# W1 by four casting transfers of the GpSimd queue, w sent to all partitions, one PSUM pool, free order of the second product, stores on two queues, and a new written order

## The chip, the cores and the metric

The kernel runs on one core of one Trainium2 chip. A core has five engines with an instruction stream each: TensorE (PE, matmuls and transposes into PSUM), VectorE (DVE), ScalarE (ACT), GpSimd (POOL) and SyncE (SP, which here only issues DMA transfers). Sixteen DMA engines move data between HBM and SBUF; transfers are issued by SP, ACT and POOL, each on a queue of its own. The metric is device time in microseconds for one execution, as the median of several runs; smaller is better.

## The reference

Two layers run one after the other. The first is a linear attention with a decaying state, for 4 batches, 8 heads, 768 steps and 48 channels per head:

```
state = 0                                       # (B, H, D, D)
for t in range(768):
    cur   = (u * k_t) outer v_t
    y_t   = r_t @ (state + cur)
    state = w * state + k_t outer v_t           # w: one factor per head and channel
```

The second takes the 3072 rows of 384 numbers that result, and computes

```
h   = max(x @ w_in, 0)                          # w_in: 384 x 2048, called W1 here
out = (h * h) @ w_out                           # w_out: 2048 x 384, called W2 here
```

All inputs and the output are float32 in HBM.

## The kernel before, in words

**Blocks.** The time axis is cut into chunks of 128 steps. A block i is one chunk of one batch (batch i % 4, chunk i // 4), 24 in all. In a block the decay is put into scaled copies of r and k, so that the loop becomes matrix products. These are the steps of block i, by the names that the code and the written order use:

- `ld.r.i`, `ld.k.i`, `ld.v.i`: loads, 192 KB each, in rows of 48 floats (192 bytes).
- `rh`, `kh`: r and k times powers of w, to bfloat16 (`Wt`, `Wk` are these powers, from `logw`). `P0`, `P1`, `du`, `dv`: the term with u (r times k, times u, summed per head, times v). `vb`: v in bfloat16.
- The transposed r and k come in one of two ways: `T` (eight transposes on PE into a PSUM bank) and `Tc` (a copy to SBUF), or `XB`, one transposing DMA issued by SP.
- `A`: scores, eight matmuls into two banks; `Bm.i.0`, `Bm.i.1`: masked copies; `Y`: scores times v plus (from chunk 1 on) r times the state; `xs`: Y plus the u term, to bfloat16.
- `U`: the update of the state; `S0`, `ts`, `S`: the state itself.
- x is transposed for the second layer either by `X` (PE) and `xTc` (a copy), or by `xX`, a transposing DMA on SP.

**Groups.** The second layer works on groups of blocks: group 0 is block 0, group 1 is block 1, group 2 is blocks 2 and 3, group 3 is 4 and 5, and so on to group 12. `F1.g.s` is one bank of the first product for group g (for two blocks: 6 matmuls of 256 columns, s from 0 to 7; for one block 12 matmuls of 128 columns, s from 0 to 3). `re` (relu) empties the bank, `sq` squares. `F2.i.q` is a quarter q of the second product for block i: 4 matmuls of 384 columns into the block's bank. `os` copies the finished bank to SBUF, `out` stores it.

**Weights.** W1 lies in SBUF as eight pieces of 256 columns, W2 as four pieces (q). `lW.0.s` loads a float32 piece of W1 on SP into one of four staging buffers, `cW.0.s` casts it (on ACT, one on POOL). `W.0.2` and all of W2 (`W.1.q`) come by a DMA that casts on its way, which POOL issues. In most pieces two neighbouring rows of W2 lie together, with the columns of W1 permuted to match. `w` sends the decay to four partitions, and `shw` on DVE spreads it to all 128.

**What sets the order.** Nothing is scheduled by a tool. `ORDER` is a list written out by hand: a step such as `F1.1.0:P/0` names what, the engine (P, D, A, G for POOL, S) and the buffer numbers. Each engine runs its own steps strictly in the order of the list, and waits where an input is missing or a buffer is still in use. `Z.n.b` are n filler matmuls on PE. The transfers issued by SP and ACT share eight semaphores in turn, so that each waits until the transfer eight places before it in the list has landed. The eight PSUM banks are fixed in three pools: 4 for the attention, 2 for F1, 2 for F2's results.

The lines touched are in `POOLS`, `ORDER`, `HELD`, `bank`, `weights`/`rows2`, `w`/`shw`, `lW`/`cW`/`W`, `F1`, `re`, `sq`, `F2` and `os`.

Of the kernel before, what the change touches and what calls it, by code (L numbers as in the profile page):

```python
# [18 lines left out]
POOLS = dict(ldr=7, ldk=7, ldv=7, ws=0, wsa=4, rk=7, P0=5, dv=5, vb=8, rkT=7, bank=4, bankH=2, bankO=2, Bm=6, xs=5, xT1=2, xT2=3, xT4=1, hr=6, hq=30, os=4, ts=2)  # L19
ORDER = """  # L20
ld.r.1:S/0 w:A ld.k.1:S/0 u:S Z.48.5:P tab:A ld.k.0:S/1 ld.k.2:S/2 shw:D ld.r.0:S/1 logw:A ld.r.2:S/2 Wt:A/0 P0.1:D/0
Wk:A/1 lW.0.6:S/0 kh.1:D/0 ld.v.1:S/0 rh.1:D shu:D ld.k.3:S/3 T.1:P/0 kh.0:D/1 Z.16.5:P P1.1:G Tc.1:A/0 kh.2:D/2
rh.0:D ld.v.3:S/1 WtS:A rh.2:D P0.2:G/1 A.1:P/1/2 WkS:A T.0:P/3 lW.0.1:S/1 Z.16.5:P P1.2:D ld.r.3:S/3 Tc.0:A/1
du.1:D/0 P0.0:D/2 cW.0.6:A ld.v.0:S/2 A.0:P/0/3 dv.1:G Bm.1.1:D/0 Z.6.5:P du.2:D/1 T.2:P/2 P1.0:G Bm.1.0:D/1
ld.v.2:S/3 Z.22.5:P Tc.2:A/2 Bm.0.0:D/2 Bm.0.1:D/3 lW.0.0:S/2 vb.1:A/0 lW.0.5:S/3 kh.3:D/3 Y.1:P/1 cW.0.1:A lW.0.7:S/0
A.2:P/0/2 xs.1:D/0 Z.4.5:P P0.3:G/3 vb.3:A/1 du.0:D/2 lW.0.4:S/1 X.1:P/3 Z.8.5:P rh.3:D wc:S xTc.1:A/0 Bm.2.0:D/4
vb.0:A/2 T.3:P/1 ld.k.4:S/4 dv.0:D Y.0:P/3 Z.13.5:P Tc.3:A/3 vb.2:G/3 Bm.2.1:D/5 P1.3:G xs.0:D/1 A.3:P/0/2 X.0:P/1
cW.0.0:A U.0:P/3 dv.2:G Bm.3.0:D/1 Z.6.7:P xTc.0:A/1 du.3:D/3 lW.0.3:S/2 F1.1.0:P/0 Bm.3.1:D/0 ld.r.4:S/4 F1.0.0:P/1
re.1.0:D/0 cW.0.7:G Y.2:P/0 Y.3:P/1 re.0.0:A/1 ld.k.5:S/5 xs.2:D/2 cW.0.5:A W.1.0:G dv.3:D F1.1.3:P/0 cW.0.4:A W.0.2:G
X.2:P/2 F1.0.3:P/1 re.1.3:D/2 ld.r.5:S/5 xTc.2:A/0 W.1.1:G U.2:P/0 xs.3:D/3 F1.0.2:P/0 re.0.3:A/3 sq.1.3:D2/0 WLcol:A  # L30
X.3:P/2 F1.1.2:P/1 re.0.2:D/4 xTc.3:A WLm:G U.3:P/1 F1.2.1:P/0 re.1.2:A/5 W.1.2:G sq.0.3:A0/1 F1.2.5:P/1 re.2.1:D/2
W.1.3:G sq.0.0:A0/2 U.1:P/2 S0.2:D re.2.5:A/3 F1.2.4:P/0 sq.0.2:D2/3 cW.0.3:A S0.0:D F1.2.7:P/1 re.2.4:D/1 sq.1.0:A0/4
F2.0.0:P/1 sq.2.5:D2/5 re.2.7:A/4 S0.3:D F1.0.1:P/0 F1.2.3:P/1 re.0.1:D/0 F2.1.0:P/0 S0.1:D re.2.3:A/3 F1.1.1:P/0
sq.1.2:D2/6 sq.0.1:D2/7 ld.k.7:S/6 F1.2.0:P/1 re.1.1:A/5 F2.0.1:P re.2.0:A/0 sq.1.1:D2/8 F1.2.2:P/0 sq.2.4:A0/9
sq.2.0:D1/10 F2.1.1:P kh.4:D/4 F1.2.6:P/1 ld.v.5:S/4 rh.4:D P0.4:D/4 F2.1.2:P ld.r.7:S/6 re.2.2:D/5 P1.4:G F2.0.2:P
re.2.6:D/1 sq.2.2:A0/11 F2.1.3:P ld.v.4:S/5 kh.5:G/5 sq.2.1:A0/12 sq.2.6:D1/13 F2.0.3:P os.1:A/0 du.4:D/4 ld.k.6:S/0
T.4:P/0 sq.2.3:A0/14 rh.5:D F2.2.0:P/0 os.0:A/1 P0.5:D/0 Tc.4:A/4 ld.r.6:S/0 T.5:P/3 P1.5:D F2.2.1:P kh.7:D/6 Tc.5:A/5
ld.v.7:S/6 A.4:P/1/2 du.5:D/0 F2.3.0:P/1 Bm.4.0:D/3 ld.k.9:S/2 A.5:P/0/3 vb.4:A/4 dv.4:G Bm.4.1:D/2 F2.3.1:P vb.5:A/5
ld.r.9:S/2 Bm.5.1:D/4 dv.5:G sq.2.7:A0/15 Y.4:P/1 Bm.5.0:D/5 F2.3.2:P rh.7:G ld.k.8:S/1 xs.4:D/4 U.4:P/2 Y.5:P/3
F2.2.2:P P0.6:G/1 ld.v.6:S/0 xs.5:D/0 X.4:P/0 ts.4:D/0 X.5:P/1 T.7:P/3 xTc.4:A/1 kh.6:D/1 ld.k.15:S/3 F2.2.3:P xTc.5:A  # L40
rh.6:D vb.7:A/6 U.5:P/2 P1.6:D F1.3.0:P/0 Tc.7:A/6 ld.k.10:S/4 ts.5:D/1 F1.3.1:P/1 kh.9:D/2 re.3.0:A/0 ld.v.9:S/2
T.6:P/0 P0.7:D/2 os.2:A/2 A.7:P/1/2 S.5:D re.3.1:A/5 ld.r.8:S/1 F2.3.3:P du.6:D/2 P1.7:G Tc.6:A/0 Bm.7.1:D/0
F1.3.3:P/0 sq.3.0:A0/16 rh.9:G ld.r.10:S/3 os.3:D/3 F1.3.4:P/1 re.3.3:A/2 Bm.7.0:D/1 A.6:P/3/0 P0.9:G/3 du.7:D/1
re.3.4:A/1 XB.9:S/1 F1.3.5:P/0 Bm.6.1:D/3 sq.3.1:A0/17 dv.7:G F1.3.6:P/1 Bm.6.0:D/2 re.3.5:A/3 F2.5.0:P/0 dv.6:G
vb.6:A/7 ld.k.12:S/5 sq.3.3:A0/18 Y.7:P/2 out.3:S kh.10:D/3 re.3.6:A/4 Y.6:P/1 ld.v.8:S/3 S.4:G xs.7:D/1 F1.3.2:P/0
sq.3.5:A0/19 xs.6:D/2 F1.3.7:P/1 ld.v.11:S/1 kh.8:D/0 re.3.2:A/0 kh.15:D/4 U.6:P/0 X.6:P/3 sq.3.2:A0/20 X.7:P/2 rh.8:D
F2.4.0:P/1 ld.r.12:S/4 re.3.7:A/5 rh.10:D F2.5.1:P xTc.6:A/2 sq.3.4:D2/21 P1.9:D xTc.7:A U.7:P/1 T.8:P/3 vb.9:A/2
out.0:S P0.8:D/4 F1.4.0:P/0 ts.6:D/1 ld.k.11:S/0 Tc.8:A/2 P1.8:G ts.7:D/0 F1.4.4:P/1 ld.r.13:S/5 du.9:D/3 re.4.0:A/2
F2.5.2:P kh.12:G/5 re.4.4:A/3 F1.4.6:P/0 ld.r.11:S/0 sq.3.6:A0/23 sq.3.7:D2/22 vb.8:G/3 du.8:D/4 A.9:P/2/0
sq.4.4:A0/24 A.8:P/1/3 S.6:G re.4.6:A/0 F2.5.3:P ld.v.10:S/5 Bm.8.1:D/4 F1.4.3:P/1 dv.8:G Bm.8.0:D/5 os.5:A/3  # L50
ld.k.13:S/6 F1.4.5:P/0 Bm.9.1:D/1 re.4.3:A/1 dv.9:G Y.8:P/3 Bm.9.0:D/0 re.4.5:A/5 XB.10:S/3 F2.4.1:P P0.12:G/0
xs.8:D/3 sq.4.0:A0/25 Y.9:P/1 vb.11:A/1 kh.11:G/1 F1.4.1:P/1 xs.9:D/4 ld.v.13:S/4 X.8:P/0 F1.4.2:P/0 re.4.1:D/4
xTc.8:A/0 ld.r.15:S/6 F2.4.2:P rh.11:D sq.4.1:A0/26 P1.12:D X.9:P/2 vb.10:A/0 F1.4.7:P/1 P0.10:D/1 ld.k.20:S/2 xTc.9:A
sq.4.5:D2/27 F2.7.0:P/0 P0.11:D/2 re.4.7:A/3 ld.v.12:S/6 U.8:P/3 P1.10:D sq.4.3:A0/28 F2.4.3:P kh.13:D/6 re.4.2:A/2
# [64 lines left out]
def kernel(  # L119
# [417 lines left out]
```

## Time and profile before

| what | value |
|---|---|
| time, median of 3 runs | 176.94 us (176.59 to 178.07) |
| profiled execution, span from first to last instruction | 175.6 us; the page gives no other time of this execution |
| PE busy | 165.1 us (94%), 624 matmuls of F1, 384 of F2, 139 fillers |
| DVE / ACT / POOL busy | 140.6 / 109.4 / 69.2 us |
| moved by DMA | 28.36 MB, mean 161 GB/s |
| SP queue (q1) / GpSimd queue (q0) | 26.10 MB in 100,360 packets / 1.77 MB in 1,744 packets |
| W2 pieces, issue to landing (median) | 10.2 us |
| loads of r, k, v, issue to landing (medians) | 4.0, 4.1, 3.8 us |
| granted TensorE clock | full, in all slices |

How to read it: the page gives for each engine its busy time, and for 40 equal slices of the span (4.4 us each here) the busy share in tenths. The chain that ended last is followed back from the last instruction, at each step to what released it. The idle time before an instruction is put down to the releaser that came last. A DMA's time to landing runs from its issue to the semaphore that tells that all of it has arrived. Times in the trace count from the first instruction.

### The profile page before, as it was taken

What the parts mean: (1) busy time and instruction counts of PE and PEld (TensorE: products, weight loads), DVE (VectorE), ACT (ScalarE), POOL (GpSimd) and SP (SyncE); (2) the same over time, 40 slices, a digit from 0 to 9 for tenths busy, and PEclk for the clock granted to TensorE, in tenths of its full rate; (3) what the DMA queues carried; (4) which work ended last, traced back from release to release, by engine and by line L of the source; (5) the groups of instructions that cost most, each with busy time, mean ns of one, the idle gap of its engine ahead of it and who ended that gap; (6) DMA issues with size and microseconds to landing.
All of it is one profiled execution on the core that took longest, in us unless ns stands there. A gap on an engine that the chain in (4) does not pass through costs nothing.

```text
span 175.6 us, 4601 instructions
## 1 busy us (share of the span) xinstructions
PE 165.1 (94%) x1813; PEld 127.0 (72%) x1813; DVE 140.6 (80%) x278; ACT 109.4 (62%) x203; POOL 69.2 (39%) x84
## 2 busy tenths in 40 slices
PE   4888797899999999999999999999999999999991
PEld 4767695666778778777767787777778677787760
DVE  4699877499899998999989899899988667853620
ACT  2479498249399987886668669669478132164401
POOL 4073582035358394926282960600960302000000
PEclk9999999999999999999999999999999999999999
DMA  5999999989899999999999979989971422110041
GB/s 105 218 217 236 315 231 187 192 166 220 163 210 106 246 207 134 232 159 242 170 162 214 212 142 223 155 203 191 199 157 26 157 90 62 33 45 0 4 169 55
DMA packets 102277, 28.36 MB, mean 161 GB/s; under 512 B 94824, under 2 KB 102256, under 8 KB 102256
## 3 DMA queue, kind: packets, MB, share of 16 engines
q1 hardware_dynamic: 100360, 26.10, 75.4%
q0 software_dynamic: 1744, 1.77, 6.1%
q8 instruction: 14, 0.23, 0.6%
q10 hardware_dynamic: 152, 0.20, 0.3%
q14 instruction: 7, 0.06, 0.1%
HBM read 20.46 MB, written 4.72 MB: 143 GB/s over the span
## 4 chain that ended last, share of the span: by engine, by line
PE 80%; DMA 10%; SPq 4%; POOL 1%; issue 1%; ACT 0%; POOLq 0%
PE bank L472 36%; PE bank L445 33%; DMA wsa<-in_moe_w_in_dram 6%; DMA W<-in_moe_w_in_dram 5%; SPq L320 4%; PE bank L376 3%; PE bank L394 2%; PE bank L392 2%; PE bank L403 2%; PE bank L363 2%; PE bank L429 1%; POOL W L262 0%; SPq L324 0%; POOL W L333 0%; ACT os L260 0%
## 5 line engine op out<-in xcount | busy, mean ns | idle before, releaser
L445 PE MATMUL bank<-xT,W 128*128 128x256 bf16 (+1 forms) x624 | 74.4, 264 | 1.6 <-ACT W L260 0.9
L472 PE MATMUL bank<-W,hq 128*128 128x384 bf16 x384 | 73.6, 326 | 1.0 <-DMA W<-in_moe_w_out_dram 1.0
L453 ACT ACTIVATE hr<-bank 128x512 bf16<-128x512 f32 x71 | 42.0, 597 | 38.9 <-PE bank L445 36.3
L445 PEld LDWEIGHTS <-W 128*128 128x128 bf16 x624 | 55.3, 98 | 12.3 <-ACT W L260 1.2
L472 PEld LDWEIGHTS <-hq 128*128 128x128 bf16 x384 | 35.6, 98 | 19.0 <-issue 1.2
L460 ACT ACTIVATE hq<-hr 128x512 bf16<-128x512 bf16 x57 | 34.7, 629 | 2.5 <-DVE hr L455 2.4
L384 DVE TENSOR_TENSOR Bm<-bank,maskJT 128x512 bf16<-128x512 f32 x48 | 31.4, 683 | 3.0 <-PE bank L376 3.0
L346 POOL TENSOR_TENSOR P<-P,ub 128x384 f32<-128x384 f32 x14 | 15.2, 1086 | 35.5 <-DVE P L342 29.8
L455 DVE TENSOR_SCALAR hr<-bank 128x512 bf16<-128x512 f32 x25 | 17.1, 689 | 11.9 <-PE bank L445 8.3
L354 POOL TENSOR_TENSOR dv<-ldv,du 128x384 f32<-128x384 f32 x19 | 16.6, 886 | 23.7 <-DVE du L349 21.6
L464 DVE TENSOR_TENSOR hq<-hr 128x512 bf16<-128x512 bf16 x35 | 15.0, 457 | 1.7 <-ACT hr L453 1.7
L411 DVE TENSOR_TENSOR xs<-bank,dv 128x384 bf16<-128x384 f32 x24 | 13.2, 553 | 2.8 <-PE bank L394 2.2
L260 ACT COPY os<-bank 128x384 f32<-128x384 f32 x18 | 8.6, 477 | 8.1 <-PE bank L472 8.1
L481 PE MATMUL bank<-identity 128*128 128x128 bf16 x139 | 11.0, 242 | 2.3 <-POOL identity masks.py:199 2.3
L349 DVE TENSOR_REDUCE du<-P 128x8 f32<-128x384 f32 x24 | 12.9, 544 | 0.2 <-POOL P L346 0.2
L342 POOL TENSOR_TENSOR P<-ldr,ldk 128x384 f32<-128x384 f32 x11 | 11.3, 1024 | 2.4 <-DMA ldr<-in_r_dram 2.4
L260 ACT COPY rkT<-bank 128x1024 bf16<-128x1024 bf16 x10 | 10.1, 1015 | 2.8 <-PE bank L363 2.7
L481 PEld LDWEIGHTS <-identity 128*128 128x128 bf16 x139 | 9.7, 111 | 2.5 <-POOL identity masks.py:199 2.3
L424 POOL TENSOR_TENSOR S0W<-ts,WLm 128x384 bf16<-128x384 f32 x7 | 7.4, 1060 | 10.0 <-PE bank L472 6.7
L394 PE MATMUL bank<-vb,Bm 128*128 128x48 bf16 x192 | 10.8, 183 | 0.4 <-ACT vb L260 0.3
L394 PEld LDWEIGHTS <-Bm 128*128 128x128 bf16 x192 | 9.5, 96 | 1.4 <-issue 0.6
L260 ACT CAST vb<-ldv 128x384 bf16<-128x384 f32 x19 | 9.6, 512 | 0.0
(61 smaller groups left out, 163.8 us busy)
## 6 DMA issues: line engine op xcount, KB each, us to landing
ldr<-in_r_dram SPq DMA_DIRECT2D x24, 192.0 KB, 4.0
ldk<-in_k_dram SPq DMA_DIRECT2D x24, 192.0 KB, 4.1
ldv<-in_v_dram SPq DMA_DIRECT2D x24, 192.0 KB, 3.8
out_dram<-os SPq DMA_DIRECT2D x23, 192.0 KB, 2.1
wsa<-in_moe_w_in_dram SPq DMA_DIRECT2D x7, 384.0 KB, 4.8
W<-in_moe_w_out_dram POOLq DMA_DIRECT2D x4, 384.0 KB, 10.2
rkT<-rk SPq DMA_TRANSPOSE x14, 4.2
W<-in_moe_w_in_dram POOLq DMA_DIRECT2D x1, 192.0 KB, 8.1
```

The costliest lines, as they stand in the source:

```text
L260: e.copy(o, a)
L346: e.tensor_mul(t, t, ub)
L354: e.tensor_mul(dvb[slot[f"dv{i}"]], loaded("v", i), t)
L384: e.tensor_mul(Bmb[slot[f"Bm{i}{h}"]], heads(bank(f"bA{i}{h}"), 128), mask_b)
L394: e.matmul(y[:, hc, D * h : D * (h + 1)], m[h][:, hc, :], vb[:, 2 * hc + h, :], start=(c == 0), stop=True, skip_group_check=True,)
L445: e.matmul(hp[:, fi, :], W1[f // 2][:, c, 128 * (f % 2) : 128 * (f % 2 + 1)], xt[:, c, :], start=(c == 0), stop=(c == CCH - 1), skip_group ...
L453: e.activation(hr, hp, AF.Relu)
L455: e.tensor_scalar_max(hr, hp, 0.0)
L460: e.activation(hq, hr, AF.Square)
L464: e.tensor_mul(hq, hr, hr)
L472: e.matmul(bank(f"bO{i}", "bO")[:, 0:d_model], hqb[slot[f"hq{g},{f // m}"]][:, at : at + L], W2[q][:, f % 4, :], start=(f == 0), stop=(f = ...
L481: e.matmul(banks[b][:, 0:128], identity, identity, start=True, stop=True, skip_group_check=True)
```

## The change

- W1 lies in four pieces of 512 columns, each loaded by one casting DMA of the GpSimd queue (786 KB read, 393 KB written). The staging buffers, `lW` and `cW` are gone, and so is the permutation; W2's pieces are read in plain rows.
- `w` goes to all 128 partitions in one DMA on ACT's queue; `shw` and the buffer `wrow` (and its memset) are gone.
- One pool of eight PSUM banks: any step may be given any bank.
- The quarters of F2 may come in any order for a block: the first in the list starts the accumulation, the fourth ends it.
- Stores are issued by SP (13) and ACT (11); before 23 and 1.
- The order is new throughout. Counts that differ: `T` and `Tc` 9 (10), `XB` 15 (14), `X` and `xTc` 8 (14), `xX` 16 (10), fillers 94 (139), `rh` on POOL 15 (6), `kh` on POOL 13 (5), `P0` on POOL 15 (11), `P1` on POOL 18 (14), `vb` on POOL 9 (3), `dv` on DVE 9 (5), `re` on DVE 32 (25), `sq` on DVE 45 (39).

The first steps of three engines, read out of the new list:

```
SP:   u r0 k0 r1 k1 v0 r2 k2 wc v1 k3 r3 v3 v2 k5 r5 v5 k6 k7 r7 r4 r6 k9 k8 k4 r9 v7 r8 r11 v10
      v6 v8 XB.4 v4 k10 v9 k13 k11 r12 r13 r10 v11 r15 out.0 k15 k16 r16 v12 r14 k14 k12 xX.9 xX.8 ...
POOL: W.0.0 W.0.2 W.0.1 W.0.3 P0.1 dv.0 P1.1 W.1.1 P0.2 dv.1 P1.2 P0.3 P1.3 W.1.2 vb.3 WLm rh.5
      kh.5 W.1.3 kh.6 P0.7 W.1.0 P0.6 rh.7 P1.7 rh.4 kh.4 kh.9 rh.8 rh.9 ...
DVE:  shu rh.0 kh.0 P0.0 rh.1 P1.0 kh.1 du.0 Bm.0.1 Bm.0.0 rh.2 xs.0 kh.2 du.1 Bm.1.1 Bm.1.0 kh.3
      xs.1 rh.3 re.0.2 du.2 Bm.2.0 dv.2 Bm.2.1 Bm.3.0 Bm.3.1 du.3 dv.3 xs.2 xs.3 S0.1 xTc.2 ...
      S0.0 sq.0.0 kh.7 rh.6 sq.0.3 P1.6 ...
PE:   Z.54 T.0 Z.18 A.0 T.1 Z.15 Y.0 U.0 Z.3 A.1 X.0 T.2 F1.0.0 Z.4 Y.1 F1.0.2 X.1 A.2 T.3 F1.1.0
      F1.0.1 A.3 U.1 F1.1.2 F1.1.1 Y.2 U.2 Y.3 F1.1.3 F1.0.3 X.2 X.3 T.5 U.3 U.5 F1.2.6 F1.2.4
      F1.2.7 F1.2.1 F1.2.2 F2.0.1 F1.2.0 T.6 F1.2.5 F2.1.1 F1.2.3 T.7 F2.1.3 F2.0.3 F2.0.2 F2.1.2
      A.5 A.7 F2.0.0 T.8 T.9 F2.1.0 Y.5 F2.2.1 F2.3.1 U.6 F2.3.0 A.6 A.4 F2.2.0 Y.7 F2.2.2 F2.3.2
      X.5 Y.4 F2.3.3 Y.6 X.4 F2.2.3 X.7 F1.3.6 ...
```

The diff without the order's lines, cut to its core:

```diff
-POOLS = dict(ldr=7, ldk=7, ldv=7, ws=0, wsa=4, ..., bank=4, bankH=2, bankO=2, ...)
+POOLS = dict(ldr=7, ldk=7, ldv=7, ..., bank=8, ...)
...
-    first = {"b": 0, "bH": POOLS["bank"], "bO": POOLS["bank"] + POOLS["bankH"]}
-    def bank(var, kind="b"):
-        return banks[first[kind] + slot[var]]
+    def bank(var):
+        return banks[slot[var]]
...
-    W1 = [const.tile([128, CCH, 256], BF16, name=f"W1_{s}") for s in range(FCH // 2)]
+    W1 = [const.tile([128, CCH, 512], BF16, name=f"W1_{s}") for s in range(FCH // 4)]
...
-    nc.vector.memset(wrow.bitcast(BF16), 0.0)
...
+    def row(a):
+        return bass.AP(tensor=a.tensor, offset=a.offset, ap=[[0, 128], [1, H * D]])
...
         def w(e):
-            e.dma_start(out=quarter_rows(wrow), in_=row4(w))
+            e.dma_start(out=wb.rearrange("p a b -> p (a b)"), in_=row(w))
...
-        def lW(e, a, s):
...
-        def cW(e, a, s):
...
         def W(e, a, s):
-            e.dma_start(out=rows2(W2[s], s) if a else W1[s], in_=weights(a, s))
+            e.dma_start(out=(W1, W2)[a][s], in_=w_out_t[s] if a else w_in_t[:, :, 512 * s : 512 * (s + 1)])
...
         def F2(e, i, q):
+            done = quarters.setdefault(i, [])
+            done.append(q)
...
-                    start=(f == 0), stop=(f == FCH - 1), skip_group_check=True,
+                    start=(f == 4 * q and len(done) == 1), stop=(f == 4 * q + 3 and len(done) == 4),
+                    skip_group_check=True,
```

## The prediction

> **What bounds the kernel now.** I read, in this order, the totals and the 40 slices, the chain that ended last, the DMA view of two windows, and SyncE's (SP's) own timeline. First the page:
>
> ```profile
> PE 165.1 (94%) x1813; PEld 127.0 (72%) x1813; DVE 140.6 (80%) x278; ACT 109.4 (62%) x203; POOL 69.2 (39%) x84
> ...
> PE   4888797899999999999999999999999999999991
> ...
> DMA  5999999989899999999999979989971422110041
> ```
>
> TensorE is full from the eighth slice to the end, and the DMA engines from the second slice to about the thirtieth. So there are two limits: matmuls after some 31 us, transfers before it. The chain tells where one hands over to the other:
>
> ```profile
> 10.53 4.45 DMA wsa<-in_moe_w_in_dram
> ...
> 16.09 5.67 DMA wsa<-in_moe_w_in_dram
> ...
> 23.53 8.06 DMA W<-in_moe_w_in_dram
> 31.63 1.50 PE bank L445 x18
> ```
>
> Until 31.63 the kernel waits for weights; from there the chain is matmuls up to 172.0. The PE rows of that chain give warm prices: F1 0.655 us for six 256-column matmuls (0.073 us for one of 128 columns, 0.88 for twelve), F2 0.65, T 0.45, A 0.275 (sixteen in 0.55), U and X 0.17, Y 0.41 (0.25 without state; an estimate from its matmul counts). Summed over the order before, without the fillers Z, that is 153.2 us, of which 139.4 stand behind 31.63. They took 140.4: +1.0. The order after sums to 151.7. The tail (last os, store, landing) is 175.6 - 172.0 = 3.6. **Nothing behind 31.63 can be won by a better order, only lost; what counts is when TensorE gets what it needs.** Timed runs lie around the profiled span by 176.94 - 175.6 = 1.3 us, which I add at the end (the page gives no other time of the profiled execution).
>
> How loads and weights share the DMA engines decides this case. These are the queues from 26 to 36 us, when five weight pieces of the GpSimd queue are under way (q0), beside the SP queue (q1); columns are packets, MB, and packet time as a share of the 16 engines:
>
> ```profile
> q0 software_dynamic: 1618, 1.60, 96.2%
> q1 hardware_dynamic: 1353, 0.26, 23.1%
> ```
>
> and from 40 to 47 us, when they are through:
>
> ```profile
> q1 hardware_dynamic: 7082, 1.34, 97.9%
> ```
>
> A load of r, k or v is 1,024 packets of 192 B. Alone, loads run at 7082/7 = 1,012 packets/us, one load in 1.0 us; beside q0 at 135 packets/us, one in 7.6 us. SP's timeline in that window shows it from the issuing side:
>
> ```profile
> 27.64 6.41 SPq L320 DMA_DIRECT2D ldv<-in_v_dram  x1
> 34.09 4.14 SPq L320 DMA_DIRECT2D ldr<-in_r_dram  x1
> ...
> 52.48 1.34 SPq L369 DMA_TRANSPOSE rkT<-rk  x1
> ```
>
> The last line, XB.9, stands behind 32 loads and all weights, and goes out at 52.48. That is the check of what follows.
>
> **The change, part by part.**
>
> *W1 on the GpSimd queue.* Removed: seven stagings (6 on ACT, 1 on POOL, 0.88 each) and seven transfers on SP. Added: three more POOL issues of 0.77, no cost there (POOL's first real work before was at 8.38). The four issues stand first on POOL, so from about 2.8 us (after maskJT). Before, the first such issue at 22.64 moved its first packet some 2.9 us later, so W1 flows from about 5.7. Its 1.57 MB (as bf16) at 1.60 MB per 10 us take 9.8 us, to about 15.5. In that time loads get some 1,300 packets. SP now begins with u, which waits for the memset on POOL until 2.44 (before, two loads went ahead of it), so the first load leaves at 2.7 instead of 0.8 and moves from about 4.2.
>
> *Block 0 and 1.* r0 and k0 are there at about 6.5, r1 during W1, k1 only at about 16.3. DVE runs kh.1 before du.0, Bm.0 and xs.0: block 0 hangs on k1. From kh.1 to xs.3 its steps sum to 13.8 us (Bm 0.683, the others 0.55 each, re 0.69): 16.9 + 13.8 = 30.7; S0.1 and xTc.2 1.0 more. F1.0.0 comes at about 20.5, as its counterpart before (20.5), and F1.2.6 at about 32. The PE work ahead of F1.2.6 is 12.9, so without a further stall A.4, which has 28.5 us of PE work ahead of it (9 T, 7 A, 5 Y, 6 U, 4 X, 8 + 8 F1, 11 F2), would come at 32 + 15.6 = 47.6. Up to here no change: 47.6 + (151.7 - 28.5) + 0.9 (its share of the +1.0) + 3.6 = 175.3.
>
> *XB.4, the term that decides.* A.4 needs the transposed block 4, which comes by DMA through XB.4, and on SP that stands behind 30 loads; all eight weight pieces are issued before it too (POOL has W.1.0 ahead of kh.4, which XB.4 reads). By the rates above: weights 3.15 MB / 0.160 = 19.7 us, carrying 19.7 x 135 = 2,660 load packets; the other 30,720 - 2,660 at 1,012 per us 27.7; from 4.2 that is 51.6. The same sum for XB.9 before (0.8 + 1.5 start, 11.1 for 1.77 MB of q0, 8.6 for 2.75 MB staged at 0.32 MB/us as between 17.8 and 21.8 us, 30.9 for 31,270 packets) gives 52.9 against 52.48 shown. XB.4 itself: transposes to landing 4.2 (median), of which I count 2.9 behind the last load's packets. **XB.4 lands at about 54.5, 6.9 us after TensorE would want it.** Bounds: 50 (loads ride more freely, no gap) and 57 (gaps as between 47 and 50, and the 5.3 that XB.9 took).
>
> *Everything after A.4*: 151.7 - 28.5 = 123.2 of matmuls, + 0.9 + 3.6. Span 54.5 + 127.7 = 182.2.
>
> *The rest.* One T and six X fewer: 0.45 + 6 x 0.17 = 1.5 us, already in 151.7 against 153.2. w to all partitions: logw at about 3.8 instead of 5.10, between -1.5 and 0; I take 0, as kh.0 waits for k0. One PSUM pool and free F2 order: at best -1.0 (the excess over the rows behind 31.63), at worst +3; 0, because the relus wait for matmuls (ACT 36.3 us in all), not matmuls for them. One XB and six xX more: DMA work of some 1 to 3 us each, most of it after 75 us; XB.11 onwards has 5 us and more to spare in the sums, xX.8 and xX.9 (F1.5, 49.9 of PE work, so 75.9) stand behind 17 loads and a store after XB.4 and land at 73 to 75: 0, at worst +3. Ten more stores on ACT: issues of about 0.53 to 1.1 us; ACT's sum falls by some 22 (fewer casts, relus, copies), so 0, at worst the third rival. POOL gets some 30 us more (kh, rh, P0, P1, about 1.05 each), 99 of 180; DVE 5 less.
>
> *Two rules of the Trainium skill beside it.* "DMA: Bandwidth & Descriptors", section on the anatomy of a GpSimd-issued DMA, prices one at 2.0 us plus bytes at 436 GB/s: the eight pieces would hold the engines 7.2 us instead of 19.7, XB.4 would land at about 42, and the forecast would be no change. The rows (W2 pieces 7.4 to 11.9 us to landing) speak against it. "TensorE: Matmul & The Clock Gate", part 1, lets the clock fall to half after an idle window of about 3.4 us, and T.1 waits from 9 to 17 us here; F1 of groups 0 and 1 (7.0 us) would take 14. The first 48 fillers show such a start (4.55 us, 95 ns each; later 22 in 1.39). All of it lies ahead of A.4, in the shade of XB.4.
>
> **Rivals.** *Same (the stall is hidden or the shares are kinder):* XB.4 lands by 47.6 to 49.7; span 175.3 to 177.4, 176.6 to 178.7 in time. For it: loads could ride at up to one packet per q0 packet. Against: before's own XB.9. *Faster:* W1 flows in the background at the loads' cost of nothing. Then k1 is there at 8.5, kh.1 at 9.0, all of DVE's start 7.3 us earlier, F1.2.6 at 25, XB.4 lands at 38 (30 loads at 1.0 us from 4.2, and 2.9), ahead of A.4 at 40; span 25 + 138.8 + 4.5 = 168.3, time 169.6. It decides once loads keep 1,000 packets/us while q0 flows; the window from 26 to 36 us shows 135. *Slower still:* the chain of late loads goes on. POOL and DVE steps for blocks 6 to 13 wait in order for loads (rh.6, P0.13), and each store on ACT must first see the eighth transfer before it land, with relus queued behind; one to three such waits of 2 us, or xX.8 late: time 186.5 to 192.
>
> **How the numbers follow.** Forecast 182.2 + 1.3 = 183.5 (179.5 to 186.5 by XB.4's bounds, rounded): 0.65. Slower still 0.22, same 0.07, faster 0.06. The range 178.5 to 190 leaves out faster, same and the far end. Runs of this kernel tell 1% from no change (175.2 to 178.7): faster 0.06, same 0.07, slower 0.87.
>
> **What would show it.** In the profile after: q0 at some 90% from 6 to 15 us with q1 near 135 packets/us; block 0's du waiting for k1 at about 16; F1 first at about 20 to 21; gaps of PE before T.6, T.9 and A.4, the last ended by XB.4's transpose at about 54; PE full behind it. Wrong if PE is full from 35 on, or if F1 starts before 15 us; also if the weights move much faster than 0.16 MB/us when they come in rows of 2 KB.

## The result, and the profile after

| | time, median (lowest to highest) | ratio to before, 95% interval | span of the profiled execution |
|---|---|---|---|
| before | 177.05 us (176.59 to 178.07, 4 runs) | | 175.6 us |
| after | 197.2 us (195.05 to 198.8, 4 runs) | 1.1043 [1.0966, 1.112] | 194.0 us |
| forecast | 183.5 us (178.5 to 190) | | 182.2 us |

The change makes the kernel 10% slower. The direction was forecast, the size was not: the span is 11.8 us longer than the forecast's, and the time lies outside the range. Most kernels here have some slower executions too; the ratios compare the faster ones alone (195.05 and 195.73 us after, some 18 us above before), and the spans of e2, e3 and e10, which were profiled in slower ones, are not used.

Totals and slices of the page after (a slice is 4.85 us here):

```profile
PE 167.9 (87%) x1742; PEld 127.5 (66%) x1742; DVE 155.2 (80%) x268; ACT 90.6 (47%) x167; POOL 103.8 (53%) x116
...
PE   5631998749979995999998899999999999999992
...
DVE  4305779699999989898999999999989964897510
...
PEclk9995599996999999699999999999999999999999
DMA  4999999999999961299667599858899222401033
```

PE, full from the eighth slice on before, has holes until past the middle of the span. DVE is at eight or nine tenths from about 40 to 155 us, though it has ten instructions fewer than before (268 against 278): 155.2 us against 140.6. And the granted clock, full in every slice before, falls to half or 0.6 in four slices.

Groups of the page after: instructions, busy us and mean ns, then the idle time before them. First the masked copies with an input in PSUM (0.683 us each before, 0.677 now), then the squares on DVE whose inputs are both in SBUF (0.457 before, 0.771 now):

```profile
L359 DVE TENSOR_TENSOR Bm<-bank,maskJT 128x512 bf16<-128x512 f32 x48 | 30.7, 677 | 0.2 <-PE bank L351 0.2
L439 DVE TENSOR_TENSOR hq<-hr 128x512 bf16<-128x512 bf16 x36 | 27.2, 771 | 0.3 <-ACT hr L428 0.2
```

One form did not change and the other became two thirds longer. The timeline of DVE from 38 us (start, duration) shows the worst case:

```profile
38.77 4.23 DVE L439 TENSOR_TENSOR hq<-hr 128x512 bf16<-128x512 bf16 x1
42.92 0.55 DVE L311 TENSOR_TENSOR rk<-ldk,Wkhat 128x384 bf16<-128x384 f32 x1
43.39 0.54 DVE L314 TENSOR_TENSOR rk<-ldr,Wt 128x384 bf16<-128x384 f32 x1
```

and POOL's timeline at the same time:

```profile
38.85 1.02 POOL L317 TENSOR_TENSOR P<-ldr,ldk 128x384 f32<-128x384 f32 x1
39.82 1.00 POOL L314 TENSOR_TENSOR rk<-ldr,Wt 128x384 bf16<-128x384 f32 x1
40.77 0.99 POOL L321 TENSOR_TENSOR P<-P,ub 128x384 f32<-128x384 f32 x1
41.72 0.98 POOL L314 TENSOR_TENSOR rk<-ldr,Wt 128x384 bf16<-128x384 f32 x1
```

One square takes 4.23 us, ten times its 0.41, about as long as POOL runs four instructions back to back. Behind it on DVE stands rh.6 (the third line), on which T.6, and with it all of TensorE, waits until 44 us. Its load was not late: POOL's P0.6, which reads r6 too, starts at 38.85 (the first line of POOL's).

**The lag.** One number per step makes the runs comparable: the start of a PE step less the sum of the PE work listed ahead of it, at the warm prices of the forecast and without fillers. It is what TensorE has lost up to there. Before, it reaches 17.8 us at 31.6 us and grows by only 0.8 in all that follows. Worked out from each trace (the time of the step is in brackets; A.4 is given for the new order alone, where it is the step that XB.4 feeds; the end is the last PE step):

| run | blocks 0 and 1: first Y | around 50 us | A.4 | end |
|---|---|---|---|---|
| before | 12.7 (14.6) | 17.8 | | 18.6 |
| after | 19.8 (21.0) | 27.4 (F1.2.3, 46.7) | 29.6 (58.1) | 38.6 |
| e1, POOL sets memory only | 22.2 (23.3) | 28.1 (F1.2.3, 47.4) | 28.7 (57.2) | 31.7 |
| e4, W1 later | 12.6 (13.8) | 26.5 (T.7, 46.4) | 31.5 (60.0) | 40.6 |
| e5, as e1, with POOL's waits | 19.7 (20.9) | 25.7 (T.9, 50.3) | 26.4 (54.9) | 33.9 |
| e6, e5 without W2's transfers | 19.2 (20.4) | under 22 | 19.6 (48.1) | 25.4 |
| e12, squares on ACT | 19.6 (20.8) | 26.3 (T.7, 46.2) | 28.1 (56.6) | 33.8 |
| e13, e12 with block 6 later | 19.9 (21.0) | 29.8 (A.5, 52.7) | 32.9 (61.5) | 38.2 |
| e14, e13 with W1 later | 13.1 (14.2) | 28.0 (A.5, 51.0) | 31.4 (59.9) | 37.9 |
| e8, before with W1 alone | 22.0 (23.9) | 24.8 (F1.1.0, 28.7) | | 25.4 |
| e9, e8 spread out | 13.8 (15.7) | 17.7 | | 17.9 |

Lag, work (151.7 or 153.2) and tail (3.6) give the span within 0.5 us: 38.6 + 151.7 + 3.6 = 193.9 for after, 194.0 measured. So 20 us more of lag are to be explained (less 1.5 us of work): 7 in the first two blocks, 2.5 more up to 47 us, and 10 more behind that. The forecast's own lag is 26.0 at A.4 and 26.9 at the end: of the 11.7 us that it lacks, 3.6 lie ahead of A.4 and 8.1 behind it.

### The profile page after: what moved, and what is told of

It is laid out like the page before. It is cut to its first block, busy times and chain, and to the rows that moved or that the text cites. A ratio compares the mean times of both kernels' runs of the same rounds, so it can differ in the third digit from the quotient of the medians.

```text
span 194.0 us, 4450 instructions
## 1 busy us (share of the span) xinstructions
PE 167.9 (87%) x1742; PEld 127.5 (66%) x1742; DVE 155.2 (80%) x268; ACT 90.6 (47%) x167; POOL 103.8 (53%) x116
## 5 line engine op out<-in xcount | busy, mean ns | idle before, releaser
L428 ACT ACTIVATE hr<-bank 128x512 bf16<-128x512 f32 x64 | 36.8, 597 | 39.6 <-PE bank L420 29.0
L435 ACT ACTIVATE hq<-hr 128x512 bf16<-128x512 bf16 x51 | 30.6, 627 | 12.4 <-DVE hr L430 12.2
L439 DVE TENSOR_TENSOR hq<-hr 128x512 bf16<-128x512 bf16 x36 | 27.2, 771 | 0.3 <-ACT hr L428 0.2
L430 DVE TENSOR_SCALAR hr<-bank 128x512 bf16<-128x512 f32 x32 | 21.4, 682 | 4.2 <-PE bank L420 4.1
L317 POOL TENSOR_TENSOR P<-ldr,ldk 128x384 f32<-128x384 f32 x15 | 16.4, 1093 | 13.2 <-DMA ldk<-in_k_dram 12.1
L329 POOL TENSOR_TENSOR dv<-ldv,du 128x384 f32<-128x384 f32 x15 | 13.1, 878 | 18.7 <-DVE du L324 18.7
L321 POOL TENSOR_TENSOR P<-P,ub 128x384 f32<-128x384 f32 x18 | 19.5, 1088 | 2.6 <-DVE P L317 2.2
L314 POOL TENSOR_TENSOR rk<-ldr,Wt 128x384 bf16<-128x384 f32 x15 | 16.8, 1125 | 3.9 <-DMA ldr<-in_r_dram 3.9
L338 PE MATMUL bank<-identity,rk 128*128 128x128 bf16 x72 | 6.4, 240 | 13.8 <-DVE rk L311 8.8
L311 POOL TENSOR_TENSOR rk<-ldk,Wkhat 128x384 bf16<-128x384 f32 x13 | 15.3, 1178 | 3.7 <-DMA ldk<-in_k_dram 3.7
L338 PEld LDWEIGHTS <-rk 128*128 128x128 bf16 x72 | 5.1, 108 | 14.9 <-DVE rk L311 9.1
L324 DVE TENSOR_REDUCE du<-P 128x8 f32<-128x384 f32 x24 | 12.8, 540 | 0.0
L369 PE MATMUL bank<-vb,Bm 128*128 128x48 bf16 x192 | 11.7, 186 | 0.5 <-DVE Bm L359 0.4
```

The costliest lines, as they stand in the source:

```text
L311: e.tensor_mul(rk[slot[f"rk{i}"]][:, 1, :, 0:D], loaded("k", i), early("WkP") if i < EARLY else Wkhat)
L314: e.tensor_mul(rk[slot[f"rk{i}"]][:, 0, :, 0:D], loaded("r", i), early("WtP") if i < EARLY else Wt2)
L317: e.tensor_mul(P0b[slot[f"P{i}"]], loaded("r", i), loaded("k", i))
L321: e.tensor_mul(t, t, ub)
L428: e.activation(hr, hp, AF.Relu)
L430: e.tensor_scalar_max(hr, hp, 0.0)
```

## The experiments

Ratios are to the kernel before, timed beside each.

### e1_memset: POOL without reads of SBUF

```diff
         def P0(e, i):
+            if e is nc.gpsimd:
+                e.memset(P0b[slot[f"P{i}"]], 0.001)
+                return e.memset(P0b[slot[f"P{i}"]], 0.001)
             e.tensor_mul(P0b[slot[f"P{i}"]], loaded("r", i), loaded("k", i))
...
```

and the same in rh, kh, P1, dv, vb and S.

> The kernel after, in which every step of rh, kh, P0, P1, dv, vb and S that runs on POOL is replaced by two memsets of its result (so these products are left out of what is computed); POOL stays busy for a similar time but reads nothing from SBUF. Theory 'port' (a DVE step whose two inputs both lie in SBUF is held up while a POOL step reads SBUF, and the added POOL work made DVE the bound): the mean of hq<-hr on DVE falls from 771 ns to about 430, DVE's busy time from 155 to about 137 us, and the time from 197 to about 184 to 187. Theory 'queue' (the late loads of the start and their consequences are the whole of it, DVE only fills the time): the time stays at 194 to 198.

Measured: 187.86 us (187.43 to 188.83), ratio 1.0572 [1.0496, 1.0647]; DVE's group of squares in it:

```profile
L460 DVE TENSOR_TENSOR hq<-hr 128x512 bf16<-128x512 bf16 x36 | 14.5, 419 | 1.9 <-ACT hr L449 1.8
```

Every form of DVE is back at its shortest, and some 8 us of the time are gone (0.047 of the ratio). But this POOL waits for no load either, and is busy for 83.5 us instead of 103.8, so the run does not say which of these made the gain; e5 does.

### e2_shares: the kernel after with the engines of before

```diff
-... kh.5:G P0.7:G P0.6:G rh.7:G rh.4:G ...
+... kh.5:G P0.7:D P0.6:G rh.7:G rh.4:D ...
```

Each rh, kh, P0, P1, dv, vb, S, re, sq and os of the new order goes to the engine that it had before (167 steps).

> The kernel after, with each step of rh, kh, P0, P1, dv, vb, S, re, sq and os given to the engine that has it in the kernel before (POOL gets its old share, DVE and ACT theirs); order, buffers and transfers stay. Port: hq<-hr back to below 500 ns, DVE about 143 us, time 185 to 190. Queue: 194 to 198.

Measured: 214.29 us (212.68 to 216.44), ratio 1.202 [1.1917, 1.2123]. Both theories missed. DVE's timeline and its idle time say why:

```profile
33.58 0.56 DVE L312 TENSOR_TENSOR rk<-ldk,Wkhat 128x384 bf16<-128x384 f32 x1 [2.21 <-DMA ldk<-in_k_dram]
39.76 0.56 DVE L318 TENSOR_TENSOR P<-ldr,ldk 128x384 f32<-128x384 f32 x1 [5.62 <-DMA ldr<-in_r_dram]
40.23 0.68 DVE L360 TENSOR_TENSOR Bm<-bank,maskJT 128x512 bf16<-128x512 f32 x1
```

P0.7, which the new order lists early, now stands on DVE ahead of the masked copies of block 2, and waits there 5.62 us for r7. TensorE waits 9.42 us for that copy. The order was written for these shares: steps whose loads come late were on POOL, where nothing urgent stood behind them. Shares cannot be taken back alone, and the run tells nothing on the price of POOL's reads.

### e3_before_pool: the kernel before with POOL's shares of after

```diff
-... kh.4:D/4 ... rh.4:D ... rh.5:D ... kh.7:D/6 ...
+... kh.4:G/4 ... rh.4:G ... rh.5:G ... kh.7:D/6 ...
```

Only rh, kh, P0, P1, vb, dv and S move (76 steps), in the old order.

> The kernel before, with only the steps rh, kh, P0, P1, vb, dv and S given to the engines that they have after (POOL gets the larger share); weights, order, buffers and transfers stay. Port: hq<-hr rises from 457 to 600 ns or more, DVE's busy time does not fall although it has fewer steps, and the time rises by 5 to 12 us to 182 to 189. Queue: 176 to 178.

Measured: 183.96 us (181.46 to 184.66), ratio 1.0259 [1.014, 1.0378]. DVE's squares in it:

```profile
L464 DVE TENSOR_TENSOR hq<-hr 128x512 bf16<-128x512 bf16 x35 | 19.3, 583 | 2.0 <-ACT hr L453 2.0
```

0.583 us instead of 0.457 with nothing changed but POOL's share, and DVE, with 23 instructions fewer (255), is busy for 143.5 us instead of 140.6. The shares of after cost the kernel before 3%, where TensorE had nothing to win from them. How much of that is POOL's reads and how much POOL's own lateness, this run does not tell.

### e4_w1_late: the kernel after, W1's last three quarters later

```diff
-... W.0.0:G ... W.0.2:G ... W.0.1:G ... W.0.3:G ... P1.1:G ...
+... W.0.0:G ... P1.1:G W.0.2:G W.0.1:G W.0.3:G ...
```

> The kernel after, with three of the four W1 pieces issued behind P1.1 on POOL instead of ahead of P0.1, so that the first loads share the DMA engines with one piece only. Both theories: k1 some 6 us earlier than its 17.9, F1.0.0 at 16 to 19 instead of 23.8. Queue: the time falls by 6 to 10 us to 187 to 191. Port: what the start wins is lost again behind it, the time falls by less than 4, to 193 to 197.

Measured: 197.54 us (196.95 to 198.44), ratio 1.1109 [1.1016, 1.1202]: no gain. kh.1 came at 11.0 us instead of 17.9 and the first lag fell by 7 us, but at T.7 1.5 us of it was left (46.4 us instead of 47.9) and at A.4 nothing: F1.0.2 had waited 2.47 us for a piece of W1, T.3 3.14 us for r3.

### e5_memset_waits: e1, with POOL's waits kept

```diff
         def P0(e, i):
+            if e is nc.gpsimd:
+                e.tensor_mul(P0b[slot[f"P{i}"]][:, 0, 0:2], loaded("r", i)[:, 0, 0:2], loaded("k", i)[:, 0, 0:2])
+                e.memset(P0b[slot[f"P{i}"]], 0.001)
+                return e.memset(P0b[slot[f"P{i}"]], 0.001)
...
```

> The kernel after, in which each of POOL's rh, kh, P0, P1, dv, vb and S is a multiplication or copy of two columns (so that it waits for the same loads and the same results as before) and then two memsets of the tile; the products themselves are left out. POOL is as busy as in the kernel after, but hardly reads SBUF. It closes a gap of e1_memset, whose POOL waited for no load. Theory (POOL's reads hold up DVE): hq<-hr back at 410 to 430 ns, 186.5 to 190 us, as e1_memset. Rival (what e1_memset won came from POOL not waiting for late loads): hq may be short, but the time is 192 to 197.

Measured: 190.86 us (190.02 to 192.74), ratio 1.0762 [1.0624, 1.09]: between the two, nearer the theory. POOL is as busy as in the kernel after (107.2 us against 103.8), DVE 131.8 instead of 155.2:

```profile
L467 DVE TENSOR_TENSOR hq<-hr 128x512 bf16<-128x512 bf16 x36 | 14.4, 417 | 0.2
```

POOL's reads of SBUF cost the kernel after some 5 us: 0.028 of the ratio, and 4.6 us between the spans (194.0 and 189.4). Another 3 us lie between e5 and e1: steps of POOL that wait in their order for a load or a result. That second figure is weak, as the two intervals just overlap.

### e6_no_w2: e5 without W2's transfers

```diff
         def W(e, a, s):
+            if a:
+                return
...
+    for t in W2:
+        nc.vector.memset(t, 0.001)
```

> e5_memset_waits, in which W2 is set by four memsets at the start instead of being fetched: 1.57 MB of the GpSimd queue's transfers, some 9.8 us of the 16 DMA engines, are left out, and with them the meaning of F2's results. Theory (what is left behind e5 is the early part: blocks 5 and 6 wait for r5, k5 and r6, which share the DMA engines with all weights): T.6 ends at 34 to 37 instead of 44 to 45, and the time is 177 to 182. Rival (the order on the engines costs it, whatever the transfers do): T.6 comes earlier, but the time stays at 184 or more.

Measured: 182.21 us (181.61 to 185.25), ratio 1.0249 [1.0183, 1.0314]. T.6 ends at 37.6 us instead of 42.3 in e5; the time falls by some 9 us, to a shade above the theory's 182. So most of what is left behind e5 goes when 9.8 us of transfers (an estimate, from 0.16 MB/us) are taken away. Not all of that is the change's doing, as the kernel before moves W2 too; the same transfers were not taken out of that kernel, so the share of the change stays open.

### e7_pairs: two engines side by side

```
meet()                                  # DVE, POOL and ACT wait for one another
for j in range(16):
    nc.gpsimd.tensor_mul(Pb[j % 2], lr, Wt)
for j in range(12):
    nc.vector.tensor_mul(hq[j % 2], hr, hr)
```

> Not the reference's computation: a kernel that runs a few short series, DVE and POOL (or ACT and POOL) released together in each. Series 1: DVE hq<-hr (128x512 bf16, both inputs SBUF) alone. 2: beside POOL memsets. 3: beside POOL multiplications of 128x384 f32 back to back. 4: DVE multiplication of 128x384 f32 alone, 5: beside POOL's. 6: DVE addition with one input in PSUM alone, 7: beside POOL's. 8: ACT squares beside POOL's. Theory (an instruction of POOL that reads SBUF and a DVE instruction with both inputs in SBUF shut each other out): 410 to 420 ns in 1 and 2, at least 800 ns a piece in 3 (or one DVE instruction held through many of POOL's), 4 at 550 and 5 above 900, 6 and 7 alike within 5%, 8 undisturbed at 550 to 650. Rival (only bandwidth is shared): 3 and 5 longer by at most a third, no instruction held for more than one of POOL's.

The squares on DVE of series 1, 2 and 3; min/median/max in ns (the twenty-first of the second line belongs to the first series):

```profile
L70 DVE TENSOR_TENSOR hq<-hr x12: 411/412/417, 5.2 to 8.9; 128x512 bf16<-128x512 bf16 x12
...
L70 DVE TENSOR_TENSOR hq<-hr x21: 411/412/414, 8.9 to 15.7; 128x512 bf16<-128x512 bf16 x21
...
L70 DVE TENSOR_TENSOR hq<-hr x12: 417/1210/1210, 27.2 to 38.1; 128x512 bf16<-128x512 bf16 x12
```

Three times as long beside multiplications. The second series does not show what memsets do, as they did not run beside the squares. POOL's timeline:

```profile
9.43 6.70 POOL L66 COPY bp<-bd 128x16 f32<-128x16 f32 x1 [3.45 <-DVE bd L65]
16.08 10.85 POOL L82 MEMSET P<- 128x384 f32 x30
```

The small copy ahead of them, which reads SBUF, stood for 6.70 us until the twenty squares were through (9.29 to 16.07). That memsets do not disturb is shown by e1: of its 36 squares 15 overlap a memset of POOL in time, and all take 414 to 426 ns.

POOL's multiplications take 1.168 us in series 3, against 0.985 alone. The additions with one input in PSUM took 0.679 us alone and 0.679 beside POOL, ACT's squares 0.612. One expectation missed, and taught more: the multiplications of 128x384 f32 on DVE stayed at 0.546 us in the series that was to have POOL's beside them. POOL's timeline shows that here, too, a copy stood and the multiplications came later:

```profile
50.99 5.62 POOL L66 COPY bp<-bd 128x16 f32<-128x16 f32 x1 [4.78 <-DVE bd L65]
56.58 1.94 POOL L79 TENSOR_TENSOR P<-lr,Wt 128x384 f32<-128x384 f32 x2
```

A copy of sixteen columns, 0.2 us alone, stood for 5.62 us until the whole row of twelve DVE instructions was through (50.85 to 56.55). So the two shut each other out, one instruction at a time in one series, for a whole run of instructions in the other.

### e8_w1_alone: the kernel before with W1's new route

```diff
-... lW.0.6:S/0 ... cW.0.6:A ... lW.0.1:S/1 ...
-... P1.1:G ... W.0.2:G ...
+... W.0.0:G W.0.3:G W.0.2:G W.0.1:G P1.1:G ...
```

> The kernel before with one part of the change: W1 as four quarters, cast by the GpSimd queue, issued ahead of P1.1 on POOL; seven stagings on SP and their casts are gone, everything else keeps its order. Theory (the route itself costs little, it is the order of loads and steps put around it that loses the start): the lag of TensorE ends at 16 to 20 us instead of 17.8, time 175 to 180. Rival (the route itself takes the loads' bandwidth at the start and so loses the 8 to 10 us of the early part): 184 to 190.

Measured: 183.83 us (183.29 to 186.37), ratio 1.0342 [1.0273, 1.041]. DVE's timeline at the start:

```profile
8.06 0.54 DVE L335 TENSOR_TENSOR rk<-ldk,bank 128x384 bf16<-128x384 f32 x1
13.54 0.56 DVE L335 TENSOR_TENSOR rk<-ldk,bank 128x384 bf16<-128x384 f32 x1 [4.94 <-DMA ldk<-in_k_dram]
17.72 0.55 DVE L338 TENSOR_TENSOR rk<-ldr,bank 128x384 bf16<-128x384 f32 x1 [3.62 <-DMA ldr<-in_r_dram]
```

kh.2 waits 4.94 us and rh.0 another 3.62, TensorE 8.31 us in one piece, and the first F1 starts at 28.7 us instead of 20.5. From there TensorE is full: 6 us are lost and stay lost. The time lies between the two, just below the rival's range. Whether it is the route or its place at the front, the next run shows.

### e9_w1_spread: the same, issued later

```diff
-... W.0.0:G W.0.3:G W.0.2:G W.0.1:G P1.1:G ... dv.1:G ... P1.0:G ... P0.3:G ...
+... P1.1:G W.0.0:G ... dv.1:G W.0.3:G ... P1.0:G W.0.2:G ... P0.3:G W.0.1:G ...
```

> e8_w1_alone with the four issues spread over POOL's order (behind P1.1, dv.1, P1.0 and P0.3, so from about 9 us instead of 2.7), everything else as before. Theory (what e8 lost is the moment: W1 on the wire while k0, k2 and r0 are still to come): kh.0 waits no longer, T.0 is back at 9 to 10 us, F1.1.0 at 20 to 23, time 175 to 179. Rival (the GpSimd queue's form of the transfer costs the loads as much wherever it stands): 182 to 185.

Measured: 176.43 us (174.89 to 179.69, 10 runs), ratio 0.9885 [0.9834, 0.9936]: 1% faster than the kernel before, and far faster than the kernel after. Totals and slices of its page:

```profile
PE 165.3 (95%) x1813; PEld 128.0 (73%) x1813; DVE 140.6 (80%) x278; ACT 105.2 (60%) x197; POOL 70.8 (41%) x86
...
PE   4978979999999999999999999999999999999991
```

The first F1 is at 20.5 us again, and F1.0.1, which before waited for its weights until 31.63, starts at 30.8. So the casting transfers are no loss in themselves: they may not go ahead of the first loads.

### e10_w_alone and e11_stores_sp: two parts that cost nothing

```diff
-            e.dma_start(out=quarter_rows(wrow), in_=row4(w))
+            e.dma_start(out=wb.rearrange("p a b -> p (a b)"), in_=row(w))
...
-... shw:D ...
```

> The kernel before with one part of the change: w is sent to all 128 partitions by its DMA, and the memset and the shuffle on DVE are gone. Theory (as predicted: the chain to 31.63 us is transfers of weights, w is not on it): 0, within 1%. Rival (Ln, Exp and kh.1 move forward by 1.3 us and all of the start with them): 1 to 1.5 us faster.

Measured, in the kernel before: 179.08 us (177.6 to 182.93), ratio 1.0056 [1.0015, 1.0097]. No gain, as forecast.

```diff
-... out.2:A ... out.3:A ... out.5:A ...
+... out.2:S ... out.3:S ... out.5:S ...
```

> The kernel after with all stores issued by SP, at the same places of the order. Theory (as predicted: the stores on ACT cost nothing): within 1% of the kernel after, 195 to 199. Rival (ACT's waits for the eighth transfer before, 3.6 us in all, hold up relus): 192 to 195.

Measured, in the kernel after: 196.79 us (195.85 to 200.35), ratio 1.1071 [1.0994, 1.1148], against 1.1043 of the kernel after. The stores on two queues neither cost nor win.

### e12_squares_act: the kernel after, its squares off DVE

```diff
-... sq.0.0:D2/4 ... sq.0.3:D2/5 ... sq.2.3:D2/10 ...
+... sq.0.0:A0/4 ... sq.0.3:A0/5 ... sq.2.3:A0/10 ...
```

> The kernel after with DVE's 36 squares whose inputs are both in SBUF moved to ACT at the same places, nothing else changed: DVE has 27 us less to do, ACT 22 us more (113 of 194). Theory (DVE held up by POOL paces what lies behind A.4, and ACT's squares are not held up): 188 to 193, the lag of TensorE grows by 3 to 6 us behind A.4 instead of 10. Rival (DVE is not what paces it): 195 to 200, or above where ACT gets in its own way.

Measured: 191.2 us (189.99 to 191.73), ratio 1.0764 [1.0694, 1.0834]: some 5 us won (0.028 of the ratio) by moving 36 instructions to an engine that POOL does not hold up. The stretch from 60 to 145 us of both kernels, busy us of PE, PEld, DVE, ACT, POOL, then clock, DMA share and GB/s; after:

```profile
60.00:145.00 85.00, 79.94 (x820) 60.35 (x819) 80.97 (x131) 43.74 (x85) 61.63 (x61) 0.98 0.77 161
```

and e12:

```profile
60.00:145.00 85.00, 81.64 (x851) 61.77 (x850) 74.89 (x121) 54.97 (x108) 62.23 (x63) 1.00 0.87 171
```

DVE falls from 95 to 88% busy, and TensorE does more work in the same time. The time was as expected, and so was the lag: behind A.4 it grows by 5.7 us (28.1 to 33.8) instead of 9.0. Of the 4.8 us of lag that the run wins, 1.5 lie ahead of A.4. DVE's other steps with two inputs in SBUF are held up as before (P1 1.24 to 1.34 us at 44 and 49 us).

### e13_block6_later and e14_and_w1_late: mending the order by hand

```diff
-... rh.6:D ... P1.6:D du.6:D/4 ... kh.8:D ...
+... kh.8:D rh.6:D P1.6:D du.6:D/4 ...
-... T.6:P/7 F1.2.5:P/6 F2.1.1:P/1 F1.2.3:P/4 ... F2.1.2:P Tc.6:A/6 ...
+... F1.2.5:P/6 F2.1.1:P/1 F1.2.3:P/4 ... F2.1.2:P T.6:P/7 Tc.6:A/6 ...
```

> e12_squares_act with block 6 asked for later: on DVE rh.6, P1.6 and du.6 go behind kh.8, on TensorE T.6 behind F2.1.2, on ACT Tc.6 behind it. SP's order and all transfers stay. Theory (the order on DVE and TensorE asks for r6 before it can be there): TensorE does not stop for 2.6 us at T.6, the lag behind T.7 is 24 to 25 instead of 26.3, and the time is 187 to 190. Rival (the waits move on to the next late load or to XB.4): 190.5 to 193.

Measured: 195.1 us (194.09 to 197.01), ratio 1.0966 [1.0878, 1.1054], worse than e12 by 4 us. DVE's timeline:

```profile
46.48 0.55 DVE L325 TENSOR_REDUCE du<-P 128x8 f32<-128x384 f32 x1 [4.16 <-POOL P L322]
47.99 0.56 DVE L318 TENSOR_TENSOR P<-ldr,ldk 128x384 f32<-128x384 f32 x1 [0.96 <-DMA ldk<-in_k_dram]
48.58 1.23 DVE L322 TENSOR_TENSOR P<-P,ub 128x384 f32<-128x384 f32 x1
49.74 1.34 DVE L312 TENSOR_TENSOR rk<-ldk,Wkhat 128x384 bf16<-128x384 f32 x1
51.00 1.34 DVE L315 TENSOR_TENSOR rk<-ldr,Wt 128x384 bf16<-128x384 f32 x1
```

rh.6 (the last line) now stands behind du.7, which waits 4.16 us for POOL's P1.7, behind a late load, and behind two steps held up by POOL at twice their length. T.6 stops TensorE for 3.64 us in its new place instead of 1.79 in its old one. The rival was right, and past its own end: the wait moved on and grew.

Then W1's last three quarters again behind P1.1:

```diff
-... W.0.0:G ... W.0.2:G ... W.0.1:G ... W.0.3:G ... P1.1:G ...
+... W.0.0:G ... P1.1:G W.0.2:G W.0.1:G W.0.3:G ...
```

> e13_block6_later with W1's second to fourth quarter issued behind P1.1, as in e4_w1_late. Theory (e4's gain at the start was lost again to DVE's hold-ups and to T.6's wait): now it stays, 182 to 187. Rival (the bytes ahead of blocks 1 to 6 are the same, and the order of the kernel after asks for them all before it has other work): within 1.5 us of e13.

Measured: 194.34 us (193.16 to 195.04), ratio 1.0938 [1.0861, 1.1016], 0.8 us from e13: the rival. As in e4, 7 us won at the first Y are lost again: 1.5 are left at A.4, 0.3 at the end.

## Why the prediction was wrong

**What held.** Before is bound by TensorE behind 31.63 us and by transfers ahead of it: e8 loses 6 us at the start and keeps every one, e9 wins 0.8 us there and keeps it. W1's flow was right too. The queues of the kernel after from 6 to 15 us (packets, MB, share of the 16 engines):

```profile
q0 software_dynamic: 1403, 1.39, 93.0%
q1 hardware_dynamic: 1631, 0.31, 27.0%
```

That is 0.154 MB/us against the forecast's 0.160, and 181 load packets per us against 135. Block 0 waited for k1 as said, until 17.9 us instead of 16.3, and F1.0.0 came at 23.8 instead of 20.5: the list of waits of PE in the kernel after (us in total, times, longest) begins with kh.1, in the first line:

```profile
PE bank L338 <- DVE rk L311: 8.8, 2, 7.0
PE bank L338 <- DVE rk L314: 2.8, 1, 2.8
```

w to all partitions (e10) and the stores on ACT (e11) cost nothing, as forecast. The PSUM pool and the order of F2 were not tried by themselves.

**The step that failed most: "The rest", with "POOL gets some 30 us more ...; DVE 5 less" at a cost of nothing.** POOL did get 34.6 us more (103.8 against 69.2). But DVE, at some 136 by the forecast, took 155.2. The same DVE instructions take 131.8 us when POOL hardly reads SBUF (e5), so 23.4 us of DVE's time are waiting inside its instructions; 12.8 of them are the squares. This cost some 5 us by e5 and as much by e12, and with POOL's own waits, the other cost of giving it more work, 8 by e1: of the 12 us by which the forecast fell short, the larger part.

Most of the shortfall lies where the forecast was surest, in "everything after A.4": 182.2 - 54.5 = 127.7 us by the sum, 194.0 - 58.1 = 135.9 measured. The sum took TensorE to be the only limit there, and DVE, at 80.97 of 85 us (76.56 before), was the second. In lag, the kernel after loses 9.0 us behind A.4, e12 5.7, e5 7.5 and e1 3.0. So POOL's reads alone do not make up this stretch: in e5 DVE waits there 5.2 us for dv from POOL instead, and only when POOL waits for nothing either is most of it gone.

The trace before had shown it. The squares of the kernel before, min/median/max:

```profile
L464 DVE TENSOR_TENSOR hq<-hr x35: 411/418/1212, 24.4 to 166.1; 128x512 bf16<-128x512 bf16 x35
```

One form with one shape, and a longest three times its shortest; the forms with an input in PSUM, 684 to 692 ns, have no such spread. A price taken from a mean hides a wait inside the instruction, and such a wait grows with the other engine's share (a mean square from 0.457 to 0.583 us in e3). The Trainium skill states the mechanism, in "SBUF — State Buffer", section "Who interferes with whom": a VectorE instruction with two inputs in SBUF contends with a GpSimd instruction that reads SBUF, not with one that only writes it, and the page calls the shared pair of ports an exclusive lock. e7 agrees for multiplications (1.21 us a square instead of 0.41), e1 and e5 for memsets (0.42). The forecast weighed two other rules and passed over this one, which spoke against the change.

**The deciding term, XB.4, was well timed and did not decide.** Forecast: it lands at 54.5 us and TensorE waits for it. SP's timeline has it (start, us):

```profile
49.90 1.95 SPq L344 DMA_TRANSPOSE rkT<-rk  x1
```

Such transposes land 3.1 to 4.4 us after their issue, so at 53.0 to 54.3. But TensorE came to A.4 only at 58.1, without a wait for it. The sum before it had TensorE free from 32 to 47.6; in truth F1.2.6 came at 36.2 and T.6 stood until 44.0. "Without a further stall" was the failing condition. Block 5 waited for a load: POOL's rh.5 stood 3.88 us for r5, the fourteenth load of SP's row, until 33.1, and T.5 came at 35.4. The rates for that were in the forecast; they were applied to XB.4 alone, and not to every load that an earlier PE step needs. Block 6 waited for DVE: r6 was there, and rh.6 stood behind the square of 4.23 us. In e5 and e12, where no square stood so long, rh.6 waited 3.27 and 4.40 us for r6 itself and ran at 41.33 and 42.34 instead of 43.39, so the exclusion lengthened a stall that a late load alone makes in those two runs. Two figures of the forecast do not follow from its own sum, without changing the outcome: XB.4's bounds give 179.0 to 186.0 us, not 179.5 to 186.5, and eight pieces in 7.2 us would land XB.4 at 43.7, not 42.

**The clock.** The forecast put a half clock "in the shade of XB.4". There was no such shade. The first low slices (0.50 from 13.61 to 23.85 us) stand behind T.1's wait of 7.0 us and end as F1.0.0 begins. For a later one, stages of the kernel after (clock is the third number from the end) and of e12 in the same stretch; after:

```profile
43.50:48.50 5.00, 4.51 (x30) 3.14 (x31) 4.93 (x10) 2.60 (x6) 2.10 (x2) 0.66 0.95 177
```

e12:

```profile
43.50:48.50 5.00, 4.08 (x35) 2.83 (x34) 4.68 (x7) 3.69 (x6) 5.00 (x6) 1.00 0.83 163
```

After T.6's wait of 2.83 us the granted clock was 0.50 from 44.33 to 47.74 us (0.66 in the mean of the row), after e12's 1.79 us it stayed full. The Trainium skill, "TensorE: Matmul & The Clock Gate", part 1, names an idle window of about 3.4 us; here 2.83 us of pure idleness, with a half-finished T.6 ahead of it, were enough, and a wait of 1.96 us ahead of U.8 was followed by 0.50 from 78.47 to 81.88. Over these two stretches the lag grows by 1.6 us (F1.2.5 to T.7) and 2.1 us (U.8 to F1.4.4). e5 and e12 have neither: their clock is full from 21.8 us on, so what they win contains this loss, which was not measured by itself.

**The rivals.** "Slower still" named the right family, late loads that chain on, and had 0.22; its 186.5 to 192 fell short by 3 to 5 us, since it too had DVE free. "Faster" was wrong for the reason given, as e8 shows: loads do not keep their rate while the casting queue flows.

**The sum as measured.** Of the 18 us between the kernels, some 5 are POOL's reads. Some 3 are POOL's own waits, with the doubt told above. The other 10 are left in e1. e6 shows that the time moves with the transfers, which points to W1 put first and twenty loads called for early; that these make up the 10 us is argued, not shown, and so is how they share. The one PSUM pool and the free order of F2 may have a part in them. In the old order W1 first costs 6 us; in the new order issuing it later wins nothing (e4, e14), since blocks 2, 3, 5 and 6 then wait for the same bytes, and one attempt to call for block 6 later made it worse (e13).

## What to carry to other kernels

Before moving elementwise work from VectorE to GpSimd, look at the spread of VectorE's durations within one form and shape: if forms with two inputs in SBUF spread and those with a PSUM input do not, work given to GpSimd is paid for by VectorE (23.4 us of waiting inside its instructions here), and work given to ScalarE is not (its squares took 0.612 us beside GpSimd's multiplications). A large transfer goes behind the first loads that the compute engines need, not ahead of them: the same four transfers cost 6 us when issued at 2.7 us and won 1% when issued from 9.5 us on. And where an order is written by hand, the engine of a step and its place belong together: the engines of before in the new order took 214 us, more than either kernel, and the engines of after in the old order 184, more than the kernel before.

## What was not expected of the hardware

- The exclusion between VectorE and GpSimd is not shared out fairly. In e7 one pairing alternated (each VectorE square 1.21 us), another let twelve VectorE instructions through while a GpSimd copy of 0.2 us stood for 5.62. In the kernel after one VectorE square stood for 4.23 us through four GpSimd instructions.
- GpSimd memsets do not take part in it: in e1 36 VectorE squares, 15 of them beside a memset, took 414 to 426 ns each, as against 412 alone.
- Beside the casting queue's packets of some 1 KB, loads in packets of 192 bytes move at about one packet for each of the other's: 1,631 against 1,403 in 9 us, 0.31 MB against 1.39.
